# Summing the words of the weight tiles on VectorE, without the copies that held their loads, in a new order of operations

## The chip, the cores and the metric

One core of a Trainium2 chip runs the whole program: PE (TensorE), DVE (VectorE), ACT (ScalarE), POOL (GpSimd) and SP (SyncE, which issues nearly all DMAs). The metric is the device time of one execution in microseconds (us); lower is better. A time is compared as the median of several executions; the profile is one further execution, with a time of its own.

## The reference

A recurrent attention (delta rule) over 768 steps for 4 batches of 8 heads of 48 columns, and then a gated feed-forward network (FFN) on its 3072 rows of 384 columns:

```
for t in range(S):                       # S = 768
    y[:, :, t] = einsum('bhd,bhde->bhe', q[:, :, t], state)
    v_old = einsum('bhde,bhd->bhe', state, kt)          # kt: k scaled to length 1
    state = state + bt * einsum('bhd,bhe->bhde', kt, vt - v_old)
x = y as (3072, 384)
xn = x / sqrt(mean(x * x) + 1e-06) * rms_g
g = xn @ w_gate                          # 384 x 1536
out = (g * sigmoid(g) * (xn @ w_val)) @ w_out           # 1536 x 384
```

The three weight matrices arrive as 64-bit floating point numbers; everything else is 32-bit.

## The kernel before

The sequence is cut into 12 chunks (c = 0 to 11) of 64 steps. For a chunk, k is loaded, its lengths are taken (`norms`), k is turned and multiplied with itself (`prep`), a triangular system is solved (`invert` for c = 0 and 1, which works on PE with small steps on DVE and ACT between; a longer elimination on DVE for the others), and then `recur` multiplies the solution with v, updates the state and gives the chunk's rows x. The FFN of the chunk follows: `ffn_plain` for c = 0 and 1, and from c = 2 on `ffn` and `down`, which use fewer products on sums of the weights that `factors` and `out_factors` make on DVE.

**The order is written out.** Nothing is scheduled while the program runs. The function first adds some 2790 operations to a `Plan` (`P.add(engine, duration, function, priority, reads, writes)`). `Plan.run` then takes their order from the string `ORDER`: each pair of its characters is the number of an operation in the order in which they were added. Each engine gets its own operations in that order and works through them without overtaking; waits between engines follow from what is read and written. `P.add` of a DMA (helper `dma`, L394 to L400) puts it into SP's queue, where an issue that has to wait holds back every issue behind it. The durations (`0.9`, `work=1.02`, `after=...`) are what a search outside the kernel used to find the string, and inside the kernel they decide one thing: how many filler matmuls (`filler`, L1613) are put into PE's gaps before 110 us. A filler multiplies the identity by itself into a bank that nobody reads.

**The weights.** `weights(first, last)` loads 18 tiles of 768 KB, n = 0 to 17, each a piece of w_gate (wg), w_val (wv) or w_out (wo). In order: n0 wg and n1 wv (FFN columns 0 to 255 of the first half), n2 wg, n3 wv, n4 wo, n5 wg, n6 wv, n7 wo, n8 wo; then the same nine for the second half, n9 to n17. A tile lands in one of 7 buffers `raw` (the list `RAWS` says which; 0 to 2 lie in `more`, 3 and 4 in `hf`, 5 and 6 in `wsum`), so a later tile's load waits until ACT has read the earlier one. The 64-bit numbers become 32-bit ones in four instructions: ACT scales the high words into `cva` (L496) and the low words into `cvb` (L497), DVE shifts the high ones by 3 bits (L491), and POOL adds the two as unsigned words into the weight tile (L494, the function `added`).

**The copies.** `hold()` adds three copies of one column on POOL (L514): of `u_` into `raw[4]`, of `ms[0]` into `raw[5]`, of `xp1` into `raw[6]`. Nobody reads what they write. Since the loads of n4, n5 and n6 overwrite these tiles, they wait until chunk 0 has come to u, to ms and to x.

**Lines that the steps below name.** PE: L696 (k with itself), L803 and L822 (the two products of each step of `invert`), L1155 (solution by v, c below 2), L1135 and L1192 (y and the state's update), L1058 (state by q or k), L1280 (turning x), L1352 and L1334 (FFN up and down, c below 2), L1447 and L1504 (FFN up and down from c = 2), L584 (scores). These run the array with 128 rows, or cut into pieces of 64 rows (L696, L803, L822, L584, L1058, L1073, L1121, L1135, L1155, L1192) or of 32 (L1000, L1020). DVE: L715 (aligning for `invert`), L759 and L765 (its steps), L606 and L608 (lengths of k), L1235 (mean of squares of x), L1253 (scaling x), L1361 (silu times value, into `hf`). ACT: L573 (copies of turned k and q), L789, L1164 (u), L1217 (squares of x), L1289 (x by rms_g), L1318 (state out of PSUM), L1360 (silu). POOL: L629 (root of the length, `pow`), L840 (k by its length), L1083, L1242 (root for x).

## Time and profile before

| what | us |
|---|---|
| time, median of 3 executions (663.59 to 665.52) | 664.23 |
| the profiled execution's own time | 664.82 |
| its span, first to last instruction | 663.1 |
| PE busy with matmuls | 650.8 |
| DVE, ACT, POOL busy | 539.4, 296.8, 167.5 |
| POOL busy in the 18 sums L494 | 32.8 |
| ACT in the 36 scalings L496 and L497 | 32.9 |
| DVE in the 18 shifts L491 | 13.1 |
| filler matmuls on PE (L1615, 48 of them) | 18.4 |
| first FFN matmul of chunk 0 starts | 42.46 |
| last matmul ends | 658.85 |

The span is one execution by the hardware profiler; the time around it is some 1.7 us longer (664.82 against 663.1). The granted clock of PE is 1.00 in every stretch of this profile. A matmul's end is modelled, so consecutive matmuls overlap a little in the timeline. An idle time in square brackets is that of the engine just before the instruction, with what ended it.

### The profile page before, as it was taken

The page shows a single profiled execution, that of the slowest core. Times are in us where ns is not written, and L with a number is a line of the kernel's source. Part 1 is how long each engine was busy: PE and PEld are TensorE (multiplying, and loading weights), DVE is VectorE, ACT ScalarE, POOL GpSimd, SP SyncE. Part 2 cuts the span into 40 slices and gives each one's busy share as a digit, 9 for nine tenths or more (in the row PEclk, how much of TensorE's full clock was granted, in tenths as well). Part 3 has the DMA queues.
Part 4 walks back from the last instruction along what each step waited for, and adds up shares of the span by engine and source line. Part 5 has one row for each costly group of instructions (what it writes and reads, how often), then busy time and mean ns, then how long its engine had stood idle before and what let it go on. Part 6 is the DMA issues. An engine that isn't in the chain of part 4 may idle for free.

```text
span 663.1 us, 23217 instructions
## 1 busy us (share of the span) xinstructions
PE 650.8 (98%) x9930; PEld 602.4 (91%) x9930; DVE 539.4 (81%) x1129; ACT 296.8 (45%) x705; POOL 167.5 (25%) x222
## 2 busy tenths in 40 slices
PE   8989999999999999999999999999999999999997
PEld 5677887887899999999999899999999989999997
DVE  5868998998889887899888897999798789458373
ACT  4677744235236244445245445445345244353230
POOL 2274982040600610510500510520510301000000
PEclk9999999999999999999999999999999999999999
DMA  8779754746466376485385456386355233210101
GB/s 215 192 222 280 181 147 74 121 109 120 105 97 108 76 120 130 73 155 93 52 134 121 81 96 120 84 148 102 67 102 104 61 60 78 53 50 1 25 1 25
DMA packets 270423, 69.36 MB, mean 105 GB/s; under 512 B 257456, under 2 KB 262576, under 8 KB 270000
## 3 DMA queue, kind: packets, MB, share of 16 engines
q1 hardware_dynamic: 269280, 67.68, 50.8%
q8 instruction: 78, 1.28, 0.8%
q10 hardware_dynamic: 1040, 0.20, 0.2%
q14 instruction: 25, 0.20, 0.1%
HBM read 49.76 MB, written 22.02 MB: 108 GB/s over the span
## 4 chain that ended last, share of the span: by engine, by line
PE 89%; DMA 4%; DVE 3%; ACT 1%; issue 1%; POOL 1%; SPq 1%; ACTq 0%; POOLq 0%; DVEq 0%
PE bank L1447 40%; PE bank L1504 21%; PE bank L1352 7%; PE bank L1334 4%; PE bank L584 3%; PE bank L1058 3%; PE bank L1135 2%; PE bank L1121 2%; DMA k<-in_k_dram 1%; DMA vt<-in_v_dram 1%; PE bank L1192 1%; DMA wsum<-in_moe_w_val_dram 1%; PE bank L1000 1%; PE bank L1020 1%; SPq L398 1%
## 5 line engine op out<-in xcount | busy, mean ns | idle before, releaser
L1447 PE MATMUL bank<-xf,w_in 128*128 128x128 f32 x1440 | 178.4, 276 | 0.4 <-ACT tmp L1459 0.4
L1447 PEld LDWEIGHTS bank<-xf,w_in 128*128 128x128 f32 x1440 | 169.3, 192 | 2.2 <-ACT tmp L1459 0.6
L1457 DVE TENSOR_TENSOR tmp<-tmp,bank 128x512 f32<-128x512 f32 x180 | 120.4, 682 | 42.0 <-PE bank L1447 32.1
L1447 PE MATMUL bank<-xf,more 128*128 128x128 f32 x960 | 122.5, 276 | 0.0
L1447 PEld LDWEIGHTS bank<-xf,more 128*128 128x128 f32 x960 | 114.8, 192 | 0.8 <-issue 0.2
L1459 ACT COPY tmp<-bank 128x512 f32<-128x512 f32 x120 | 68.1, 586 | 100.7 <-PE bank L1447 71.2
L1463 ACT ACTIVATE tmp<-tmp 128x256 f32<-128x256 f32 x120 | 48.1, 415 | 72.5 <-DVE tmp L1457 72.2
L951 DVE TENSOR_REDUCE acc<-acc 128x30 f32<-128x90 f32 (+4 forms) x150 | 70.9, 473 | 5.2
L1504 PE MATMUL bank<-wo_sb,hf 128*128 128x192 f32 x360 | 64.3, 330 | 0.0
L1504 PEld LDWEIGHTS bank<-wo_sb,hf 128*128 128x128 f32 x360 | 58.0, 190 | 0.9
L945 DVE TENSOR_TENSOR acc<-acc,at 128x60 f32<-128x60 f32 (+4 forms) x150 | 52.2, 348 | 4.7 <-POOL at L925 1.5
L890 POOL TENSOR_TENSOR at<-at,beta_b 128x256 f32<-128x256 f32 (+3 forms) x32 | 19.6, 643 | 139.2 <-DMA at<-dkk 139.2
L1464 DVE TENSOR_TENSOR hf<-tmp 128x256 f32<-128x256 f32 x120 | 46.7, 417 | 2.6 <-ACT tmp L1463 2.4
L629 POOL TENSOR_TENSOR knrm<-ksum,half 128x16 f32<-128x16 f32 x11 | 32.1, 2922 | 34.8 <-DVE ksum L608 34.4
L971 POOL COPY acc<-acc 128x128 f32<-128x128 f32 x40 | 17.1, 459 | 84.0 <-DVE acc L951 83.6
L1334 PE MATMUL bank<-wo_sb,hf 128*128 128x384 f32 x96 | 34.5, 492 | 1.4 <-POOL w_in L494 1.4
L1352 PE MATMUL bank<-xp,w_in 128*128 128x256 f32 x144 | 33.1, 382 | 0.0
L1352 PE MATMUL bank<-xf,w_in 128*128 128x256 f32 x144 | 33.0, 382 | 0.0
L1352 PEld LDWEIGHTS bank<-xf,w_in 128*128 128x128 f32 x144 | 27.0, 190 | 4.5
L1304 DVE TENSOR_TENSOR xf<-xf 128x256 f32<-128x256 f32 (+1 forms) x70 | 28.4, 440 | 3.2 <-ACT xf L1274 2.7
L1352 PEld LDWEIGHTS bank<-xp,w_in 128*128 128x128 f32 x144 | 26.9, 190 | 4.5
L1241 POOL TENSOR_SCALAR ms<-ms 128x2 f32<-128x2 f32 x11 | 2.7, 245 | 102.0 <-ACT bank L1229 101.9
(208 smaller groups left out, 1029.9 us busy)
## 6 DMA issues: line engine op xcount, KB each, us to landing
at<-dkk SPq DMA_DIRECT2D x20, 256.0 KB, 3.8
vt<-in_v_dram SPq DMA_DIRECT2D x24, 192.0 KB, 3.6
out_dram<-tmp SPq DMA_DIRECT2D x48, 96.0 KB, 2.2
k<-in_k_dram SPq DMA_DIRECT2D x23, 192.0 KB, 4.6
dks<-k SPq DMA_DIRECT2D x14, 256.0 KB, 2.9
kt<-dks SPq DMA_DIRECT2D x28, 128.0 KB, 3.4
more<-in_moe_w_gate_dram SPq DMA_DIRECT2D x4, 768.0 KB
more<-in_moe_w_out_dram SPq DMA_DIRECT2D x4, 768.0 KB
```

The lines of the kernel that those rows point to most:

```text
L629: P.add("POOL", 2.95, lambda: nc.gpsimd.tensor_tensor(out=knrm[i2], in0=ksum[i2], in1=half, op=ALU.pow), pn, r=[("ksum", i2), "half"], w=[ ...
L945: nc.vector.tensor_tensor(out=acc[:, 1:3, 0:n, j + 2 : W].rearrange("p a i t -> p i a t"), in0=acc[:, old, 0:n, j : j + 2, None].to_broadc ...
L951: nc.vector.tensor_reduce(out=acc[:, new, 0:n, j + 2 : W], in_=acc[:, lo : lo + 3, 0:n, j + 2 : W].rearrange("p a i t -> p i t a"), axis=A ...
L1304: P.add("DVE", V(128 * n), lambda dst=dst, a=a, b_=b_, op=op: nc.vector.tensor_tensor(out=dst, in0=a, in1=b_, op=op), pxv, r=[("xp", 0), ( ...
L1334: nc.tensor.matmul(po[p].t[:, 0:DM], hf[:, spot(f), 128 * p : 128 * p + 128], wo_sb[:, spot(f)], start=(f == f0), stop=(f == f1 - 1), skip ...
L1352: nc.tensor.matmul(ps.t[:, TOK * side : TOK * side + TOK], w_in[:, side, h_, 3 * t + i_, n : n + 128], x_[:, 2 * t : 2 * t + 2].rearrange( ...
L1447: nc.tensor.matmul(g.t[:, 128 * z : 128 * z + 128], fac[:, side, 128 * f : 128 * f + 128], xf[:, xs], start=(begin and z == 0), stop=False ...
L1457: P.add("DVE", V(512), lambda t=t, g=g: nc.vector.tensor_tensor(out=t, in0=t, in1=g.t, op=ALU.add), -1, r=[g], w=[tk], last=g)
L1459: P.add("ACT", A(512), lambda t=t, g=g: nc.scalar.copy(t, g.t), -1, r=[g], w=[tk], last=g)
L1463: P.add("ACT", A(256), lambda t=t: nc.scalar.activation(out=t[:, 0:256], in_=t[:, 0:256], func=ACTF.Silu), -1, w=[tk])
L1464: P.add("DVE", V(256), lambda t=t, f0=f0, p=p: nc.vector.tensor_tensor(out=hf[:, spot(f0) : spot(f0) + 2, 128 * p : 128 * p + 128], in0=t[ ...
L1504: nc.tensor.matmul(g.t[:, 0:192], a_[:, f], b_[:, f], start=(begin and f == 0), stop=(f == 5), skip_group_check=True)
```

## The change

It does five things.

1. `hold()` and its three POOL copies are removed (the plan has 2787 operations in place of 2790).
2. `added` runs on DVE in place of POOL, 18 times; the operands are the same two tiles of words.
3. The durations in the plan are other ones: DMAs of weights 3.0 or 2.6 in place of 3.06 or 2.3, of k, q and v 1.2, 1.3 or 1.35 in place of 1.02, of beta 0.3 in place of 0.2; the shift 0.7 in place of 0.57; the sum 0.97 in place of 1.55; POOL's copy L971 1.5 in place of 1.2.
4. All of `ORDER` is another string. (Below, its 42 new lines are cut.)
5. With the durations and the order, the number and places of the filler matmuls before 110 us can differ.

```
-            dma(rdst, src, 2 + 2 * n, w=[("raw", i)], dur=0.7, work=3.06 if n < HELD or n == 8 else 2.3, after=WAFTER[n] if n < len(WAFTER) else 0.0)
+            dma(rdst, src, 2 + 2 * n, w=[("raw", i)], dur=0.7, work=(3.0 if parts == 2 and dst.shape[2] == DM else 2.6), after=WAFTER[n] if n < len(WAFTER) else 0.0)
...
             def added(dst=dst.bitcast(U32), top=tiled(top), rest=tiled(rest)):
-                nc.gpsimd.tensor_tensor(out=dst, in0=top, in1=rest, op=ALU.add)
+                nc.vector.tensor_tensor(out=dst, in0=top, in1=rest, op=ALU.add)
...
-            P.add("DVE", 0.57, shifted, pr, w=cak)
+            P.add("DVE", 0.7, shifted, pr, w=cak)
             done = [("cv", n)]
-            P.add("POOL", 1.55, added, pr, r=cvk + cak, w=done)
+            P.add("DVE", 0.97, added, pr, r=cvk + cak, w=done)
...
-    def hold():
-        for n, t, key in ((HELD, u_[:, 0], ("u", 0, 0)), (HELD + 1, ms[0][:, 0], ("ms", 0, 0)), (HELD + 2, xp1[:, 0], ("x1", 0))):
-            out_, in_ = raw[n].bitcast(FP32)[:, 0:1], t[:, 0:1]
-            P.add("POOL", 0.15, lambda out_=out_, in_=in_: nc.gpsimd.tensor_copy(out=out_, in_=in_), 29, r=[key], w=[("raw", n)])
...
-        P.add("POOL", 1.2, lambda: spread(xt_, lambda d, t: nc.gpsimd.tensor_copy(out=d, in_=t), True), pi, w=["acc"])
+        P.add("POOL", 1.5, lambda: spread(xt_, lambda d, t: nc.gpsimd.tensor_copy(out=d, in_=t), True), pi, w=["acc"])
...
                 if c == 0:
                     P.slack, P.lead, P.urgent = 0.0, 0.0, 5.0
-                    hold()
                     weights(HELD, len(RAWS))
```

Both strings, turned back into operations, give each engine's queue. SP's first 30 issues (k2 and q2 are k and q, with the chunk and the half; v c.h is half h of chunk c; b is a part of beta, g is rms_g):

```
before: k0 b b q0.1 q0.0 n0 n1 n2 v0.0 q1.1 k1.1 q1.0 k1.0 n3 n8 v0.1 n7 g n4 n5 n9 n6 v1.1 n10 v1.0 b n11 b n13 k2.0
after:  k0 b q0.0 q0.1 b n1 n0 v0.0 n2 k1.0 k1.1 q1.1 n3 q1.0 n8 v0.1 n9 g n5 v1.1 n4 b n6 n7 n10 b v1.0 b n11 k2.0
```

DVE's queue from the scaling of v (L1100) to the second product with silu (L1361) of chunk 0, with S for a shift and A for a sum of a weight tile:

```
before: v L828 L632 L828 u u ms ms L1253 L1253 L1285 L1285 L705 S4 L705 L715 S5 L715 L1361 L730 L733 L749 S6 L759 L759 L1361
after:  v L828 L632 memset L828 L654 u S3 u A1 ms A0 ms L1253 A2 L1253 L1285 A3 L1285 S5 L705 L705 L715 A5 L715 L730 L1361 S4 L733 A4 L1361
```

PE's queue from the first FFN product of chunk 0 to the sixth (up f and down f are the products L1352 and L1334 of the f-th 128 columns; each up has two halves, a and b):

```
before: up0 up1 down0 up2a L1058 up2b up3 down1 up4 up5 down2 L584 L803 up6 L803 L822 L822 L803 L1073 L803 turn down3 turn L822 L822
after:  up0 up1 up2 down0 down1 up3 up4a L1058 up4b up5 L803 L584 up6a down2 L822 L803 L1073 up6b L822 L803 L803 turn down3 turn L822 L822
```

## The prediction

> **What bounds the kernel now.** First the busy times of the page: PE is busy for 650.8 of 663.1 us, so all idle time of PE is 12.3 us, and no order can win more than that plus the useless part of the fillers.

> ```profile
> PE 650.8 (98%) x9930; PEld 602.4 (91%) x9930; DVE 539.4 (81%) x1129; ACT 296.8 (45%) x705; POOL 167.5 (25%) x222
> ```

> Then the timeline of PE alone, over the whole span, kept to the lines with a bracket. From the first FFN product at 42.46 us to the last matmul at 658.85 it shows six gaps, together 4.72 us; the rest of the 12.3 lies ahead of 42.46 (1.41, 0.45, 0.18, 1.01, 0.25) and behind 658.85 (4.25).

> ```profile
> 49.27 1.53 PE L1334 MATMUL bank<-wo_sb,hf 128*128 128x384 f32 x4 [1.37 <-POOL w_in L494]
> 66.93 1.12 PE L803 MATMUL bank<-mt,m1bd 64*64 64x32 f32 x32 [0.83 <-ACT mt L789]
> 82.94 1.59 PE L1155 MATMUL bank<-r,mt 64*64 64x48 f32 x46 [0.56 <-issue]
> 372.07 0.78 PE L1058 MATMUL bank<-state,qt 48*64 48x48 f32 x35 [0.90 <-issue]
> 533.57 1.16 PE L1447 MATMUL bank<-xf,w_in 128*128 128x128 f32 x8 [0.41 <-ACT tmp L1459]
> 540.79 1.34 PE L1121 MATMUL bank<-r,mt 64*64 64x48 f32 x64 [0.65 <-ACT tmp L1463]
> ```

> Three of them, 2.76 us, lie in the stage that the change rebuilds. Third, the timelines of POOL and DVE there. DVE's own instructions grow while POOL sums words: L715 takes 0.48 us alone (a row of 0.88 for two at 10.02 us), L759 with 96 columns 0.26, here

> ```profile
> 44.02 1.83 POOL L494 TENSOR_TENSOR wo_sb<-xf,tmp 128x768 uint32<-128x768 uint32 x1 [0.88 <-ACT tmp L497]
> 44.37 1.89 DVE L715 SCALAR_TENSOR_TENSOR acc<-m1bd,side,acc 128x128 f32<-128x128 f32 x2
> 46.65 2.19 DVE L715 SCALAR_TENSOR_TENSOR acc<-m1bd,side,acc 128x128 f32<-128x128 f32 x2
> 52.81 1.64 DVE L759 TENSOR_TENSOR acc<-acc,at 128x96 f32<-128x96 f32 x1
> ```

> The second L715 ends at 48.84, the product with silu follows on DVE until 49.17, and PE, which had nothing else in its queue, starts at 49.27: the bracket names POOL, but its last sum was over at 48.69. Fourth, SP's waits up to 120 us, which show the copies:

> ```profile
> SPq L398 <- POOL hf L514: 6.9, 1, 6.9
> SPq L398 <- POOL acc L742: 3.3, 1, 3.3
> SPq L398 <- POOL rs L1242: 2.6, 1, 2.6
> ```

> n4, n5 and n6 are issued at 35.75, 38.30 and 42.49, each just behind its copy at 35.54, 38.08 and 42.28; from 32 to 36 us the DMAs move 26 and 8 GB/s. Last, the chain of waits, for what a change of row mode costs PE:

> ```profile
> 201.38 1.09 PE bank L584 x64
> 202.48 3.77 PE bank L1447 x32
> ...
> 216.30 0.92 PE bank L1058 x64
> ...
> 226.23 3.57 PE bank L1447 x32
> ```

> 64 small products take 1.09 behind large ones and 0.92 behind small ones; 32 large ones take 3.77 behind small ones and 3.57 behind large ones. Going into small pieces costs about 0.16 us, coming out 0.20.

> **The change, part by part.**

> *The sums.* POOL loses 18 sums of 1.82 us, 32.8 us in all. DVE gains 18. No row has an unsigned sum on DVE; the nearest are L1496, two inputs of 128x768 from SBUF (950 and 991 ns), and the shift L491 of the same words with one input (0.545). I take 0.97, from 0.55 to POOL's 1.82: 17.5 us. Against that, what the sums on POOL cost DVE falls away, shown by the same instruction with and without: L491 13.1 us for 18 against 9.8 at 0.545, so 3.3; L715 2.1; L608 2.3 (1.80, 0.46 and 0.44 in place of 0.11); L759 2.2; L632 1.8; L1410, L1412 and L1235 1.5. That is 13.2 us, so DVE works 4.3 us more up to 95 us. It sat idle for 9.7 us between 30 and 66, which hides it, unless a sum stands just ahead of what PE waits for.

> [...]

> *Start of the FFN.* u waits for v. v's second half is issued behind n8, and n8 for ACT's reading of n1, which stands behind L789 as before (ACT free at 23.9); v lands at 32.2 again, and L1155 starts at 33.58 again. From there DVE has A1, A0, A2 and A3 between the steps. By the rows: L1166 until 36.1, A1 until 37.05, mean at 37.2 (before 37.0 to 37.5, stretched by POOL), A0 until 38.1, mean 38.25, L1253 38.7, A2 until 39.6, L1253 40.0, then L1280 on PE 40.5, and ACT, which has n3 and n5 to scale first, ends L1289 at about 42.1 (before 42.30). On PE a filler of 1.14 us at 38.73 covers most of this wait. FFN start 42.2: **-0.2 us**, between -1.1 (that filler gone) and +2.0 (two sums in full on the path).

> *The first FFN.* Queued in front of PE's down0 are now up0, up1 and up2, 7.8 us, so until 50.0. DVE needs from 41.6: S5 0.5, two L705 1.3, L715 0.97 at 43.75 (ACT's L710 waits for its turn), A5 0.95, L715 0.95, L730 1.0, L1361 0.4, S4 0.5, L733 0.8, A4 0.95: 50.1. down0 waits 0.25 in place of 1.37. n4 is there: the copies gone, SP issues n9 at 30.4 (when ACT has read n2) and n5 at 31.5, not 38.9 and 38.3; n4 only at 36.3, since it is now queued behind half of v for chunk 1, which waits until L1155 has read v (35.5). Tiles land about 3.4 us apart (n5 5.5 us after its issue, n6 7.3 with two ahead), so n5 at 38.7, n4 at 42.5, n6 46, n7 49.3, n10 52.7. The next product that needs DVE's chain is L803 of chunk 1: PE gets to it at 63.7, DVE and ACT have it at about 60.8, so its 0.83 goes. L1058 of chunk 1 needs ACT's L1318 at 56.7; ACT has it at 56.5: I count 0.3. Then the chain of `invert`: L822 needs L797, behind A14 on DVE, at 77.75, PE is there at 77.1: 0.6. The wait of 0.56 ahead of L1155 goes. Sum: -2.76 + 0.25 + 0.3 + 0.6 = **-1.6 us**, from -2.76 (no new gap) to +3 (each of the three 1.5 us worse, an estimate from the spread of a tile's landing, 5.5 against 7.3).

> *Row modes.* Counted in both orders from the first FFN product on: PE leaves 128 rows 59 times before and 65 after, and goes between 64 and 32 rows 10 and 6 times. 6 x 0.20 + (6 - 4) x 0.16 = **+1.5 us**. Since PE is full, this is time of the path. Lower bound 0 (each switch in a gap), upper 8 x 0.20 = 1.6.

> *Late gaps.* 1.96 us behind 84 us. The order is new there too, and the plan's durations are nearer to the rows (the four copies L971 of 459 ns per chunk make 1.7; the plan had 1.2 and now has 1.5). I take a third off, **-0.6 us**, from -2.0 to +3 (one gap per two chunks as large as the 0.65).

> Removing the copies themselves, 3 x 0.19 us on POOL, is worth nothing: POOL is idle beside them. Without POOL's idle time they would cost 0.6.

> Sum: -0.2 - 1.6 + 1.5 - 0.6 = -0.9. The span becomes 662.2, the profiled run 663.9. The median shown lies 0.6 under the profiled run (664.23 against 664.82), so **663.3 us**. All low: -1.1 - 2.76 + 0 - 2.0 = -5.9; all high: +2.0 + 3 + 1.6 + 3 = +9.6.

> **The rivals.**

> *All gaps close* (659.9): the earlier tiles and a POOL that no longer blocks DVE leave no wait: -1.1 - 2.76 + 1.5 - 2.0 = -4.4, so 659.9. For it: each gap has DVE or a tile behind it. Against: three margins above are under 0.3 us.

> *ACT in order behind n10* (667.5, slower): ACT's queue has the scaling of n10 ahead of L1318, which PE needs for L1058 at 56.7. From n10's landing ACT needs 0.9 + 0.5 + 0.9 + 0.9 + 0.5 = 3.7 us. So from a landing at 53.0 on, each us later is one on PE, and DVE's L1361 and the sums behind it slip along. My estimate is 52.7. Four tiles at the 4.6 us that n4 took, in place of 3.4, land 4.8 later: 4.5 on PE less the 0.3 counted, 663.3 + 4.2 = 667.5. For it: half of v and parts of beta lie between the tiles now. Against: DMAs moved 260 to 390 GB/s whenever they had work.

> *It does not do what it says* (664.9): n4 is not earlier (36.3 against 35.75), n6 waits behind it, and the gaps stay: -0.2 + 0 + 1.5 - 0.6 = +0.7.

> **How the numbers follow.** Forecast 0.46, own range 661 to 666; all gaps close 0.25; ACT behind n10 0.23; no effect 0.06. A change of 0.3%, 2.0 us, is about what a measurement can tell from none. Faster than 662.2: 0.25 and a quarter of the forecast's 0.46, 0.36. Slower than 666.2: 0.23 and 0.02 of the last, 0.25. Within: 0.39. The range takes in both outer cases and some of the high ends: 659.5 to 668.5; beyond it lie sums of nearly all low or all high ends.

> **What would show it.** First L1352 at 42.2; L715 at 0.97 for two and L491 at 0.55 throughout; sums of 0.97 on DVE; n5's issue near 31.5, n4's near 36.3; no gap ahead of L1334 above 0.5 us; PE's busy time about 1 us higher behind 84 us for the switches. A sum above 1.2 us, a first L1352 behind 43.5, or a gap of over 1 us ahead of L1058 near 57 us would make it wrong.

## The result, and the profile after

The changed kernel takes 668.79 us (median of 12 executions, 664.40 to 672.33) against 663.65 (12 executions, 661.05 to 666.21) on the same chip: 1.0074 of the kernel before, 95% interval 1.0046 to 1.0101. It is about 5 us slower. The forecast was 663.3 with a range of 659.5 to 668.5, which the median exceeds by 0.3, and the chance given to "slower" was 0.25.

The profiled execution took 668.28 us with a span of 666.6. From its page, busy times by engine:

```profile
PE 654.8 (98%) x9930; PEld 603.8 (91%) x9930; DVE 541.7 (81%) x1147; ACT 297.4 (45%) x705; POOL 135.3 (20%) x201
```

POOL lost 32.2 us and DVE gained 2.3 (4.3 were predicted up to 95 us). PE has as many matmuls as before and is busy 4.0 us longer. The sums are what they were taken to be. Timeline of DVE, start, length, instruction:

```profile
47.47 0.96 DVE L494 CUSTOM_DVE_ANT_0 w_in<-more 128x1536 uint16<-128x1536 uint16 x1 [2.03 <-PE bank L1347]
48.34 0.61 DVE L710 SCALAR_TENSOR_TENSOR acc<-m1bd,side,acc 128x128 f32<-128x128 f32 x2
50.28 0.55 DVE L491 TENSOR_SCALAR xf<-xf 128x768 uint32<-128x768 uint32 x1
```

A sum takes 0.96 (0.97 predicted), L710 (L715 before) 0.61 for two (0.97 predicted, from a row of another shape, 128x256), the shift 0.55. Now the timeline of PE, lines with a bracket of 0.2 us and more behind 38 us (from 511 on, line numbers are 5 lower than before):

```profile
39.93 0.96 PE L1187 MATMUL bank<-u,k 64*64 64x48 f32 x50 [0.64 <-issue]
46.52 7.39 PE L1347 MATMUL bank<-xp,w_in 128*128 128x256 f32 x33 [1.95 <-issue]
84.31 1.54 PE L1150 MATMUL bank<-r,mt 64*64 64x48 f32 x45 [0.79 <-issue]
171.10 1.16 PE L1442 MATMUL bank<-xf,more 128*128 128x128 f32 x8 [0.21 <-issue]
422.31 1.52 PE L1116 MATMUL bank<-r,mt 64*64 64x48 f32 x62 [0.83 <-ACT mt L1029]
```

The two waits that the change was to remove, 1.37 ahead of the first FFN down product and 0.83 ahead of the product of `invert`, are gone. In their place stand waits that name no releaser: "issue" means that PE waited for nothing that the profile shows. The one at 46.52 is in the middle of a row of equal products: three ran at 43.65, their data was there, and the fourth came 1.95 us late.

What PE lacked, as the author reads it, was its own instructions. The page of both kernels lists a queue of the kind "instruction", q8, with 78 packets, 1.28 MB, which is 256 each of the 19993 PE instructions that the trace of before holds. The kernel's plan counts them with the line `PACKET = (130.2, 254.45, 314.0)`: by it packet k is asked for when PE reaches instruction 130.2 + 254.45 k, and needed 314 instructions later. The trace has the start of each packet's DMA, and no record of its asking. With "asked" and "needed" as the times of PE's instructions of those numbers:

```
kernel            packet  asked   started  waited  needed   PE's wait for it, and its end
before                3   32.21    34.74    2.53    37.94    none
before                4   36.82    39.64    2.82    42.25    none
before                9   76.14    80.45    4.31    81.88    0.56, until  82.94
before               45  360.02   369.73    9.71   370.38    0.90, until 372.07
after                 3   33.03    37.51    4.47    38.97    0.64, until  39.93
after                 4   36.47    44.02    7.55    42.97    1.95, until  46.52
after                 9   77.30    81.74    4.44    83.02    0.79, until  84.31
```

The times of asking and needing are estimates by that line. They count every PE instruction of the trace; counted by matmuls and weight loads alone, packet 45 of before is asked for at 361.5 (it waited 8.2) and needed at 372.11, and packet 4 of after is needed at 46.52, within 0.04 us of the instructions that stood.

Each wait ends 2.3 to 2.6 us behind the start of its packet. Over all profiles of this study there are 36 waits of 0.5 us and more on "issue" behind 28 us, and 35 of them end 2.2 to 3.0 us behind a packet's start. That ties these waits to the packets. What stood ahead of the late ones is seen in SP's queue of loads, here of the changed kernel:

```profile
31.25 0.57 SPq L398 DMA_DIRECT2D more<-in_moe_w_gate_dram  x1
32.52 0.58 SPq L398 DMA_DIRECT2D wsum<-in_moe_w_gate_dram  x1
35.36 0.62 SPq L398 DMA_DIRECT2D vt<-in_v_dram  x1
36.02 0.66 SPq L398 DMA_DIRECT2D hf<-in_moe_w_out_dram  x1
37.65 1.20 SPq L398 DMA_DIRECT2D wsum<-in_moe_w_val_dram  x1
```

n9, n5, half of v, n4 and n6 follow one another. The same queue in the kernel before:

```profile
28.29 0.47 SPq L398 DMA_DIRECT2D g_sb<-in_moe_rms_g_dram  x1
35.75 0.37 SPq L398 DMA_DIRECT2D hf<-in_moe_w_out_dram  x1
```

There nothing was issued between 28.29 and 35.75, and the DMAs moved 26 and 8 GB/s from 32 to 36 us: the copies kept the queue empty just when packet 3 was asked for, and left one tile ahead of packet 4.

### The profile page after: what moved, and what is told of

It is laid out like the page before. It is cut to its first block, busy times and chain, and to the rows that moved or that the text cites. A ratio compares the mean times of both kernels' runs of the same rounds, so it can differ in the third digit from the quotient of the medians.

```text
span 666.6 us, 23211 instructions
## 1 busy us (share of the span) xinstructions
PE 654.8 (98%) x9930; PEld 603.8 (91%) x9930; DVE 541.7 (81%) x1147; ACT 297.4 (45%) x705; POOL 135.3 (20%) x201
## 3 DMA queue, kind: packets, MB, share of 16 engines
q8 instruction: 78, 1.28, 0.9%
## 4 chain that ended last, share of the span: by engine, by line
PE 91%; SPq 4%; issue 1%; ACT 1%; DMA 1%; DVE 1%; POOL 0%; POOLq 0%; ACTq 0%
PE bank L1442 39%; PE bank L1499 19%; PE bank L1347 10%; PE bank L1329 5%; SPq L398 4%; PE bank L1609 3%; PE bank L579 3%; PE bank L1053 3%; PE bank L1130 2%; PE bank L1116 2%; PE bank L1187 1%; PE bank L817 1%; PE bank L798 1%; PE bank L556 1%; DMA yn<-dy 1%
## 5 line engine op out<-in xcount | busy, mean ns | idle before, releaser
L1442 PE MATMUL bank<-xf,w_in 128*128 128x128 f32 x1440 | 178.8, 276 | 0.0
L1442 PEld LDWEIGHTS bank<-xf,w_in 128*128 128x128 f32 x1440 | 169.3, 192 | 1.9 <-DVE tmp L1452 0.2
L1442 PE MATMUL bank<-xf,more 128*128 128x128 f32 x960 | 123.0, 276 | 0.2 <-issue 0.2
L1442 PEld LDWEIGHTS bank<-xf,more 128*128 128x128 f32 x960 | 114.7, 192 | 1.3 <-issue 0.5
L1459 DVE TENSOR_TENSOR hf<-tmp 128x256 f32<-128x256 f32 x120 | 47.6, 421 | 2.8 <-ACT tmp L1458 2.4
L885 POOL TENSOR_TENSOR at<-at,beta_b 128x256 f32<-128x256 f32 (+3 forms) x32 | 17.9, 589 | 157.7 <-DMA at<-dkk 135.9
L1347 PE MATMUL bank<-xp,w_in 128*128 128x256 f32 x144 | 33.5, 383 | 2.1 <-issue 1.9
L1347 PEld LDWEIGHTS bank<-xp,w_in 128*128 128x128 f32 x144 | 26.8, 190 | 7.2 <-issue 2.4
L1347 PE MATMUL bank<-xf,w_in 128*128 128x256 f32 x144 | 33.1, 383 | 0.0
L1347 PEld LDWEIGHTS bank<-xf,w_in 128*128 128x128 f32 x144 | 26.9, 190 | 4.5 <-issue 0.2
L1508 DVE TENSOR_TENSOR tmp<-tmp,bank 128x192 f32<-128x192 f32 x30 | 10.3, 350 | 18.4 <-PE bank L1499 15.9
```

The costliest lines, as they stand in the source:

```text
L1347: nc.tensor.matmul(ps.t[:, TOK * side : TOK * side + TOK], w_in[:, side, h_, 3 * t + i_, n : n + 128], x_[:, 2 * t : 2 * t + 2].rearrange( ...
L1442: nc.tensor.matmul(g.t[:, 128 * z : 128 * z + 128], fac[:, side, 128 * f : 128 * f + 128], xf[:, xs], start=(begin and z == 0), stop=False ...
L1459: P.add("DVE", V(256), lambda t=t, f0=f0, p=p: nc.vector.tensor_tensor(out=hf[:, spot(f0) : spot(f0) + 2, 128 * p : 128 * p + 128], in0=t[ ...
```

## The experiments

Kernels e1 to e4 and e9 to e16 keep the plan's times and banks of the kernel they come from, and its fillers but for e15: an operation is moved in the finished order, another engine called, a copy left out or put back, or a load made smaller, and nothing else. (Lines added in a kernel shift its later line numbers by 1 to 5.)

**e1, n9 behind n7** (changed kernel; 185 and 175 are the loads of n9 and n7):

```
         self.times(order, [t for t, _ in free], until if filler else 0.0)
+        order.remove(self.ops[185]); order.insert(order.index(self.ops[175]) + 1, self.ops[185])
```

> The changed kernel; only the load of n9 is issued behind that of n7 (at about 39 in place of 31.25 us), every other queue as it was. Theory (PE's supply of instructions): packet 4 of PE's instructions, asked for at 36.47 us, waited 7.55 us behind the loads of n9, n5, n4 and half of v; with one tile less ahead of it (about 3 us) it starts by 40.5 and is there before its use at 43. So PE's gaps of 0.64 (at 39.93) and 1.95 us (at 46.52) shrink below 0.2, the first L1347 is at 43.0 in place of 43.65, and the time is 2 to 2.6 us under the changed kernel's, about 666.5 or 1.004 of the kernel before. Rival (sums on DVE are late for the first FFN): the order of DVE is the same, so the first L1347 stays at 43.6 and a gap of about 2 us stays near 46, named after DVE or ACT; time as the changed kernel's, 1.007.

Measured: 665.68 us, 1.0044 (1.0020 to 1.0068). Packet 3 is in time, packet 4 still waits 5.56 us (36.09 to 41.65). Timeline of PE:

```profile
33.64 1.30 PE L1151 MATMUL bank<-vt,mt 64*64 64x48 f32 x37 [0.45 <-issue]
43.84 7.39 PE L1348 MATMUL bank<-xp,w_in 128*128 128x256 f32 x33 [0.53 <-issue]
```

The gap of 1.95 is 0.53, that of 0.64 is gone, packet 2 now costs 0.45. One load moved is worth 0.30%, about 2 us of the 5, with intervals that overlap; the theory's figure held, its "below 0.2" did not.

**e2, no copies; e3, sums on DVE; e4, both** (kernel before, its order kept):

```
-            P.add("POOL", 0.15, lambda out_=out_, in_=in_: nc.gpsimd.tensor_copy(out=out_, in_=in_), 29, r=[key], w=[("raw", n)])
+            P.add("POOL", 0.15, lambda: None, 29, r=[key], w=[("raw", n)])
...
-                nc.gpsimd.tensor_tensor(out=dst, in0=top, in1=rest, op=ALU.add)
+                nc.vector.tensor_tensor(out=dst, in0=top, in1=rest, op=ALU.add)
```

> The kernel before without its three copies, all else the same, sums on POOL included. Theory: the loads of n7, n4, n5 and n9 are now queued one behind the other from about 26 us, packets 3 and 4 of PE's instructions (asked for at 32.2 and 36.8) wait 5 us or more in place of 2.5 and 2.8, and PE shows gaps without a releaser of 1 to 4 us together ahead of 48 us; the time is 1 to 3 us above the kernel before, 1.0015 to 1.0045. Rival (the prediction on record: the copies cost nothing and their removal nothing): first L1352 at 42.4, time within 0.5 us of the kernel before.

> The kernel before with the sums on DVE at the places that they had in the order, copies kept. Theory: the copies keep the loads apart, so the packets wait under 3 us as before and no gap without a releaser over 0.3 us comes up ahead of 48 us; the sums cost 0.95 each on DVE, of which some stand ahead of what PE waits for (two between the steps from u to x): -1 to +1.5 us on the time, 0.9985 to 1.0025. Rival (the sums on DVE are the cost): the first L1352 comes 1 to 2 us later than 42.46 and the gap ahead of L1334 grows, +2 to +5 us, 1.003 to 1.0075.

> The kernel before with both: sums on DVE and no copies, in the old order otherwise. It is the change without its new order. Theory: the sum of the two runs before this one, so +1 to +4 us with the gaps without a releaser of the run without copies; what the changed kernel loses beyond that belongs to its order. Rival (the order alone is the cost): within 1 us of the kernel before.

Measured: e2 665.27, 1.0025 (1.0009 to 1.0041); e3 664.24, 1.0015 (0.9995 to 1.0036); e4 667.48, 1.0072 (1.0043 to 1.0101). Without the copies packet 3 waits 4.76 us and PE waits for it. PE's timeline and windows of e2 (length, PE busy, matmuls, granted clock, DMA share, GB/s):

```profile
38.55 1.18 PE L1192 MATMUL bank<-u,k 64*64 64x48 f32 x40 [2.31 <-issue]
```

```profile
36.00:40.00 4.00, 1.69 (x59) 0.85 1.07 354
40.00:44.00 4.00, 4.00 (x52) 0.73 0.16 29
```

The clock falls behind the wait, to a mean of 0.73 over 4 us, with the DMAs idle again; the trace's own record of the clock has 0.50 from 38.78 to 42.19. In e3 the first FFN product starts at 41.91 (42.46 before) and no wait on "issue" stands ahead of 48 us, so the rival, that the sums on DVE hold up the first FFN, fails. e4 is the change without its new order, and it is as slow as the changed kernel: the order is not needed for the loss. It is more than e2 and e3 together (0.72% against 0.40%), but the intervals are too wide to tell it from their sum. Its profile has the wait for packet 3 (1.56 us at 39.29) and two long stretches of low clock; windows of e4:

```profile
40.00:44.00 4.00, 4.00 (x38) 0.50 0.20 34
44.00:48.00 4.00, 4.00 (x78) 0.80 0.01 4
...
76.00:80.00 4.00, 4.00 (x120) 0.54 0.38 137
80.00:84.00 4.00, 4.00 (x38) 0.50 0.38 73
```

**e5, sums on DVE and two fillers**

```
+        for n, f in {267: [4], 320: [2]}.items():
+            self.ops[n].fill = f
```

> The kernel before with the sums on DVE, copies kept, and two more filler products on PE: one of 512 columns (some 0.8 us) ahead of the L803 whose gap was 1.25 us at 66.3, one of 256 columns (some 0.4 us) ahead of the L1334 whose gap was 0.85 at 48.2. They do no useful work and end before what PE waits for. Theory (PE's granted clock falls where PE is idle, and that is most of what the sums on DVE cost): the mean clock of the executions goes from 0.9967 to 0.9985 or more, the profile has no stretch below 0.98 between 60 and 76 us, and the time goes from 664.2 to 662 to 663, 0.996 to 0.999 of the kernel before, though L803 and L1334 start no earlier. Rival (an idle gap costs its own length and no more): clocks and time stay as without the fillers, 664 to 664.5.

Measured: 664.95, 1.0018 (0.9997 to 1.0038), mean clock 0.9968. A miss: in the profile both gaps are closed and no stretch of low clock is left (span 661.0), but over 12 executions clock and time are those of e3. So the gaps at 48 and 66 us are not all that lowers the clock with the sums on DVE, though in the profile of e3 the fall, from 67.76 to 71.18, stands right behind the wait of 1.25 at 66.32.

**e6 and e7, the two orders spliced** (`new` and `old` are the two orders, operations by one numbering):

```
e6: order = new[:800] + [x for x in old if x not in new[:800]]
e7: order = old[:803] + [x for x in new if x not in old[:803]]
```

> The changed kernel's order for its first 800 operations (until about 198 us on PE), and the kernel before's order for all that is left. Theory (the loss is made ahead of 100 us, by the late instructions of PE and the clock behind them): 1.004 to 1.0075, with the gaps of 0.64 and 1.95 us at 40 and 46.5 as in the changed kernel, and no gap near 421. Rival (the loss is in the later order: row modes, the gap of 0.83 at 422): within 1.002.

> The mirror of it: the kernel before (copies, sums on POOL) for its first 803 operations, then the changed kernel's order for all that is left. Theory (loss ahead of 100 us): 1.000 to 1.003, where the part above 1 is the later order's: the gap near 421 of 0.8 us in some executions and a stretch of lower clock behind it. Rival (later order): 1.004 to 1.0075.

Measured: e6 669.23, 1.0109 (1.0075 to 1.0143); e7 664.21, 1.0015 (0.9997 to 1.0033). The loss is made ahead of 198 us.

**e8, sums back on POOL in the new order** (`nc.vector` to `nc.gpsimd` in `added`)

> The changed kernel with the sums on POOL again; order, loads and fillers as they are. Theory (late instructions of PE): the gap of about 2 us at 46.5 and that of 0.6 at 40 stay, since nothing is moved on SP; the time stays 1.005 to 1.0085. Rival (sums on DVE are the cost): the gaps go or shrink by 1 us and more and the time is within 1.003 of the kernel before.

Measured: 673.10, 1.0155 (1.0125 to 1.0184). The expectation of a gap of 2 us at 46.5 was wrong: it is 0.18 there, because u came 1.58 us late and packet 4 had caught up. The rival is refuted all the more: in the new order the sums on DVE save 0.8%.

**e9, loads apart** (e1, and n4's load waits for ms, by one copy on POOL), **e10, v first** (kernel before: 15 is the second half of v, 183 is n8), **e11** (both, on the changed kernel), **e12** (e3 and e10):

```
+            if n == HELD:
+                gate = P.ops[-1]
+                gate.fn = lambda go=gate.fn, t=raw[i].bitcast(FP32)[:, 0:1]: (nc.gpsimd.tensor_copy(out=t, in_=ms[0][:, 0, 0:1]), go())
...
+        order.remove(self.ops[15]); order.insert(order.index(self.ops[183]), self.ops[15])
```

> The changed kernel with the load of n9 behind that of n7, as in the first run, and one copy put back: n4's load waits until POOL has copied a column of ms (about 38 us in place of 36.0). All other queues as in the changed kernel. Theory (late instructions of PE, and the clock behind the idle time): packet 4 of PE's instructions, asked for at 36.1 us, now finds only half of v ahead of it and starts by 39.5, so no gap without a releaser over 0.2 us is left between 38 and 50 us; the mean clock is 0.998 or more; 664 to 665.5 us, 1.000 to 1.003 of the kernel before. Rival (sums on DVE and the row modes of the new order make the loss): as in the first run, 1.004 to 1.005.

> The kernel before; only the second half of v for chunk 0 is issued ahead of n8 (at about 18.8 us in place of 24.4). In the kernel before DVE's L1100 waited 1.71 us for it, and PE's L1155 0.6 us of its 1.01 with it. Theory (the start hangs on what stands ahead in the queue of loads): L1155 at 33.1 or earlier in place of 33.58, all behind it as much earlier, 0.4 to 1.0 us, 0.9985 to 0.9995. Rival (the products and DVE's L828 end last anyway): within 0.3 us.

> Both on the changed kernel: loads apart as in the run e9, and the second half of v ahead of n8. Theory: packet 2 of PE's instructions (asked for at 27.2, started at 31.2 in the first run, behind n8 and v) is in time too, so the gap of 0.45 ahead of L1155's counterpart at 33.6 goes, no gap without a releaser over 0.2 us is left ahead of 80 us, and the time is 0.3 to 1 us below the run e9: 663 to 665, 0.999 to 1.002. Rival: as e9.

> The kernel before with the sums on DVE, copies kept, and the second half of v ahead of n8. Theory: 0.4 to 1.0 us below the run with the sums on DVE alone (664.24, 1.0015), so 663.2 to 663.9, 0.9985 to 1.001, since PE's gaps of 0.71 and 0.45 at 32.8 and 35.9 shrink and with them the lower clock. Rival (the clock falls for another reason): as that run, 1.0015, clock 0.9967.

Measured: e9 667.19, 1.0072 (1.0046 to 1.0098); e10 663.77, 1.0005 (0.9983 to 1.0027); e11 666.11, 1.0041 (1.0018 to 1.0064); e12 666.12, 1.0031 (1.0003 to 1.0059). All four missed the times that their theories gave. In e9 packet 4 starts at 39.24 and its gap is gone, as expected, but the time is not won. Timeline of PE in e9:

```profile
74.21 1.33 PE L822 MATMUL bank<-kk,x2bd 64*64 64x32 f32 x30 [1.79 <-issue]
...
175.75 1.16 PE L1447 MATMUL bank<-xf,more 128*128 128x128 f32 x8 [3.24 <-DVE ksum L608]
```

Packet 7, asked for at 64.52, started at 71.41, 2.80 ahead of the end of the first wait; the loads just ahead of it, issued at 60.74, 64.78 and 65.41, are later ones than those that were moved. Packet 19 waited 8.05 us (165.21 to 173.26) and ended the second wait 2.49 us later, whatever the bracket names. So with two packets in time, two later ones were late; that the moved loads caused this is not shown. e11 has such waits too, 0.67 at 73.17 and 1.35 at 83.32. e10 shows v off the path. e12 differs from e10 by the sums alone; it stands 0.26% higher, with intervals that overlap.

**e13 and e14, small loads; e15, small loads without fillers**

```
+            z = 32 if n > 6 else src.shape[2]
-            dma(rdst, src, 2 + 2 * n, w=[("raw", i)], ...
+            dma(rdst[:, :, 0:z], src[:, :, 0:z], 2 + 2 * n, w=[("raw", i)], ...
...
-        for w_ in n:
+        for w_ in n[:0]:
```

> The changed kernel in which the loads of n7 to n17 bring only 32 of their 256 or 384 columns of words (an eighth or a twelfth of the bytes; the rest of each tile keeps older words, so the output differs from the reference). All instructions, their order and the waits are the same; 11 loads leave the queue of DMAs nearly at once. Theory (the loss comes of PE's instructions waiting behind loads, and of the clock behind the idle time): no gap without a releaser over 0.3 us ahead of 100 us, mean clock 0.9985 or more, 660 to 662.5 us, 0.995 to 0.998 of the kernel before; most of the 5 us is gone. Rival (sums on DVE, row modes, late order are the loss themselves): 666 to 668, 1.004 to 1.0065.

> The same cut of the loads n7 to n17 in the kernel before, copies and sums on POOL kept. Theory: it had little to gain there, since its copies kept the loads apart: 661 to 663, 0.996 to 0.999, and within 1.5 us of the changed kernel with the same cut. Rival (the order and the sums lose by themselves): the changed kernel with the cut is slower than this by 3 us or more.

> The run before this one with the 48 filler products left out, which compute nothing that is used. PE is idle where they stood (18 us ahead of 95 us), and with the small loads its instructions are not late. Theory (the granted clock falls behind idle time): mean clock 0.985 to 0.993 in place of 0.998 and more, 3 to 8 us slower than with the fillers. Rival (the clock falls at random, or by load): time and clock as with the fillers, or less by a few tenths.

Measured: e13 667.32, 1.0049 (1.0022 to 1.0076); e14 661.13, 0.9966 (0.9943 to 0.9989); e15 669.61, 1.0090 (1.0061 to 1.0120). e13 against e14 came out as the rival said, 6.2 us apart. It decides less than it was made for: n4, n5 and n6, the large loads next to packet 4, stay whole, and that packet still starts at 43.61 with a gap of 1.38 us at 45.99. All other waits for packets over 0.4 us are gone. So the bytes of n7 to n17 cost about 2 us in either kernel (1.0074 to 1.0049, 1 to 0.9966), and are not what sets the two kernels apart.

e15 against e14 shows the clock. Timelines of PE, e14 and then e15:

```profile
22.06 2.06 PE L804 MATMUL bank<-mt,m1bd 64*64 64x32 f32 x64
23.92 1.13 PE L823 MATMUL bank<-kk,x2bd 64*64 64x32 f32 x32
```

```profile
23.53 3.63 PE L804 MATMUL bank<-mt,m1bd 64*64 64x32 f32 x64 [8.04 <-DVE mt L783]
26.94 3.63 PE L823 MATMUL bank<-kk,x2bd 64*64 64x32 f32 x64
31.54 3.63 PE L804 MATMUL bank<-mt,m1bd 64*64 64x32 f32 x64
```

The same 64 products take 3.63 us in place of 2.06. PE is slow from its first product on (8 of L562 take 1.94 us, 1.14 in e14) and stays so until about 44 us; from 44.66 on lengths are the old ones (L1193 1.15 in both). The fillers compute nothing and are worth 8.5 us. The window of e15 from 32 to 36 us nevertheless reads

```profile
32.00:36.00 4.00, 4.00 (x80) 1.00 0.02 4
```

with a granted clock of 1.00. The trace settles it: in e15 its first record of the clock, 1.00, begins at 44.33 us (4.6 to 8.4 in the other 19 traces), and the view prints 1.00 where there is no record. Lengths of equal groups are the surer sign.

**e16, useful work in the gaps** (kernel before, sums on DVE; 336 and 315 are halves of FFN up products)

```
+        order.remove(self.ops[336]); order.insert(order.index(self.ops[267]), self.ops[336])
+        order.remove(self.ops[315]); order.insert(order.index(self.ops[320]), self.ops[315])
```

> The kernel before with the sums on DVE, copies kept, and two products of the FFN put into PE's two largest gaps of that run: the first half of up6 ahead of the L803 that waited 1.25 us, the first half of up2 ahead of the L1334 that waited 0.85. Theory: 1.5 us of idle time becomes work, less 0.36 for two changes of row mode more, so 662.5 to 663.5 us, 0.998 to 0.9995 of the kernel before. Rival (the chains behind L803 and L1334 have no time to give): as the sums on DVE alone, 664 to 665, 1.0015.

Measured: 666.20, 1.0027 (0.9998 to 1.0056). A miss; new waits of 0.70 and 0.93 on DVE's sums and L818 came up. No version of this study beat the kernel before but e14, which leaves out most bytes of eleven loads.

**e17 and e18, the changed kernel twice more**

> The changed kernel once more, for a second profile of one execution. In the profiles so far the time from the first product with L1442's factors (L1447 in the kernel before) to the last matmul is 488 to 491 us in every kernel, and all differences lie ahead of it, 166.5 to 176.1. Theory (the loss is made in the front, and differs from execution to execution): that product starts between 169 and 176 us, with gaps that end 2.3 to 2.9 us behind the start of a packet of instructions, and 487.5 to 491.5 us follow it. Rival (the late gap near 421 with its lower clock is what costs): the product starts by 171.5 and over 491 us follow it.

> The same kernel a third time, with the same two expectations: front 169 to 176 us and 487.5 to 491.5 behind it, against a front up to 171.5 and over 491 behind it.

Measured: 666.21 and 668.80; the kernel before, run once beside them, took 667.08 with a mean clock of 0.997, so single executions serve here to compare stages, not kernels. Start of the first product with the factors in `more`, and the time from there to the last matmul's end, from the traces:

```
kernel                           front   rest       kernel                      front   rest
before                          169.47  489.36      after                      171.10  491.20
e10 old, v first                169.28  490.31      e17 after again            171.40  488.83
e7  old front, new rest         167.43  489.51      e18 after, third           174.09  488.74
e14 old, small loads            166.54  488.35      e1  n9 behind n7           169.40  488.60
e2  old, no copies              170.42  489.12      e9  loads apart            175.75  490.58
e3  old, sums on DVE            169.90  490.14      e6  new front, old rest    173.19  490.88
e4  old, both                   176.05  489.82      e8  new, sums on POOL      175.76  490.47
```

The rest is the same for both orders, 488 to 491 in all 20 profiles; the front goes from 166.5 to 176. In e18, whose time is the median of the first 12 executions, the front loses 4.6 us against the profile of before. Its timeline and windows of PE:

```profile
41.95 1.27 PE L1187 MATMUL bank<-u,k 64*64 64x48 f32 x50 [2.43 <-issue]
...
44.62 1.69 PE L691 MATMUL bank<-kt 64*64 64x64 f32 x64
...
48.37 7.39 PE L1347 MATMUL bank<-xp,w_in 128*128 128x256 f32 x33 [0.83 <-issue]
```

```profile
36.00:40.00 4.00, 3.26 (x66) 1.00 1.10 276
40.00:44.00 4.00, 2.06 (x54) 0.80 1.04 312
44.00:48.00 4.00, 3.54 (x75) 0.77 0.67 246
```

Packet 3, asked for at 33.26, started at 39.16; PE stood for 2.43 us; the clock fell behind it to 0.50 from 42.41 to 45.83, by the trace's record (L691 takes 1.69, not 1.16); packet 4, asked for at 36.70, started at 45.89. FFN start is 46.73 against 42.46.

## Why the prediction was wrong, by its steps

*Removing the copies "is worth nothing".* This is the step that failed. It costed the copies' 0.19 us on POOL and the tiles' earlier landing, and not what earlier loads do to the packets of PE's instructions (packet 3 waited 4.76 us in e2, 2.53 before). Alone it costs 0.25% (e2, interval above zero), a third of the 0.74%, and e1 and the table of packets show how. The sum had no term for PE's instructions, although the timeline of before showed two waits on "issue", 0.56 and 0.90 us; the prediction let the first "go" without naming its cause, and it became 0.79.

Behind the queued loads a packet waited up to 9.2 us in the front (packet 4 in e18, 36.70 to 45.89) and PE up to 2.43 (e18, until 41.95).

*A, start of the FFN, -0.2.* Measured +1.2 (43.65), +1.2 (43.69) and +4.3 (46.73); the prediction's own sign of error, a first product behind 43.5, is met in all three. DVE's chain did not do it: the sums were 0.95 each and u came at 36.07 against 36.41.

*B, first FFN, -1.6.* The issues came about as forecast (n9 31.25, n5 32.52, n4 36.02 against 30.4, 31.5 and 36.3), and 1.37 and 0.83 went. The small waits expected at L1058 and in `invert` did not come. The three removed were 2.76; against them stand 0.64, 1.95 and 0.79 in the first profile. "All gaps close" fails with the same numbers; "ACT in order behind n10" had about the right size, 667.5, by luck, for a wait that is not there; "it does not do what it says" (664.9) kept two gaps that went. The 260 to 390 GB/s given for busy DMAs was too narrow: the kernel before moved 195 to 388 in stretches of full share between 38 and 64 us.

*C, row modes, +1.5, and D, late gaps, -0.6.* Together +0.9 were expected; from the first product with the factors on, three quarters of the run, the time changed by -0.6, -0.5 and +1.8 in three profiles, and e7 is 1.0015 with an interval that holds 1. The +1.8 comes with one fall of the clock behind 0.83 us of waiting (0.50 from 424.23 to 427.64, by estimate half of 3.41 us lost, 1.7); windows of the first profile:

```profile
420.00:424.00 4.00, 2.91 (x129) 1.00 0.95 203
424.00:428.00 4.00, 4.00 (x16) 0.57 0.52 65
```

It did not come back in e17 and e18, though PE waited 0.74 and 0.85 us at the same place. Row modes were not tried by themselves.

*The clock* was in no term: it was 1.00 in every stretch of the one profile of before, and was taken for a constant. Mean granted clock over executions is 0.9991 before (30) and 0.9964 after (12), a difference of 0.27%, in proportion an estimated 1.8 of the 5 us. The views print means; the traces' own records of the clock are 1.00 or 0.50 in all 20, and each low one inside a run lasts 3.41 us, or twice or three times that, on a grid of 3.41 us that starts with the first record (in the first profile after, the fall begins 416.43 us behind the first record, 122 steps of 3.413). Five of the eleven:

```
kernel   clock at 0.50       PE idle in the 3.41 us ahead of it
e2       38.78 to  42.19     2.31
e18      42.41 to  45.83     2.43
e9       74.83 to  81.66     1.79
e4       76.36 to  86.60     0.45
after   424.23 to 427.64     1.09
```

In e17 PE waited 2.21 us, until 46.82, and no fall followed: the grid has a line at 45.39, with 0.78 us of the wait ahead of it and 1.43 behind. The author's estimate from this is that where the grid lies in an execution counts beside the length of a wait, which fits the differences between executions of one kernel; no run moved the grid, so it is not shown. Idle time alone doesn't tell either: e4 fell after 0.45 us, and e6 did not after 1.78. Nor did PE stand idle for the whole 3.41 us ahead of a fall: 2.43 us of waiting stood there in e18, and 1.09 in the first profile.

One low record of 3.41 us takes 0.0026 off the mean of an execution. Split by that, executions with a mean of 0.998 and more take (medians) 663.70 us before (25 of the 30 beside e3), 662.06 in e3 (4 of 12), 662.53 in e11 (3 of 12) and 665.28 in the changed kernel (2 of 12); those below take 666.02, 665.75, 667.54 and 669.62. So in these few executions the sums on DVE cost nothing where the clock holds, and most of the changed kernel's loss comes where it falls.

*What stays open.* With the sums on DVE and the copies kept, four kernels (e3, e5, e12, e16) stand at 1.0015 to 1.0031 with mean clocks of 0.9954 to 0.9968, against 0.9986 for e10 with sums on POOL; neither fillers nor work in the two largest gaps cured it. Which wait lowers the clock there isn't settled, nor whether both parts together (e4) cost more than their sum. That n4 to n6 hold up packet 4 is argued from the table and from e9, where it was in time once n4 came later; it was not tried with small n4 to n6. No variant won the whole loss back, so how it divides between late packets and the clock stays open.

## What to carry to other kernels

A load that is issued earlier was not free here: behind the earlier loads a packet of PE's instructions waited 7.55 us in place of 2.82, so look up when the instruction packets start before taking out a wait that keeps the queue empty. A wait of PE on "issue" in the profile is a term of the sum; look for the start of a packet of instructions ahead of it (2.2 to 3.0 us ahead of the end of 35 of 36 such waits here). And count an idle microsecond of PE with the clock that may follow it: in these traces a fall inside a run lasted at least 3.41 us at 0.50, and 0.45 to 2.43 us of idle time stood ahead of the five in the table.
